# Backward rows out of a Trainium2 kernel: one plain DMA on SyncE's queue in place of an indirect scatter from GpSimd

## The chip, the cores and the metric

The kernel runs on one core of a Trainium2 chip. The metric is device time in microseconds (us); the kernel before was timed three times. The profile is one further look at the same program: one execution recorded by the hardware profiler, with every instruction's start and length, every DMA packet's, and the marks that a DMA's semaphore receives as parts of it land.

## The reference

Two layers in float32. The first is a Fourier mixing of x with 8 batches, 3136 positions and 256 features; the second is a feed-forward layer with a SoLU activation and a layer norm.

```python
X = np.fft.fft(x, axis=1)            # x: (8, 3136, 256)
X = np.fft.fft(X, axis=2).real
h = X.reshape(25088, 256) @ w_in     # w_in: (256, 1024)
e = np.exp(h - h.max(-1, keepdims=True))
solu = h * e / (e.sum(-1, keepdims=True) + 1e-9)
mu, var = solu.mean(-1, keepdims=True), solu.var(-1, keepdims=True)
out = ((solu - mu) / np.sqrt(var + 1e-6) * g_ln) @ w_out   # w_out: (1024, 256)
```

The output is (25088, 256) float32, so a row of it is 1,024 contiguous bytes.

## The kernel before

**Tiling.** 3136 positions are split as 49 x 64: an output position is k1 + 49 * k2, with k1 below 49 and k2 below 64. Since the input is real, k1 and 49 - k1 share their work. A *unit* (p, k1) stands for a pair p of two batches and one k1 from 0 to 24: there are 4 x 25 = 100 units. A unit makes two output tiles of 128 rows (two batches times 64 values of k2): side 0 has the rows of k1, side 1 the rows of 49 - k1. On side 1 the rows of each batch come out with k2 running backwards. Units with k1 = 0 have only side 0, so there are 100 tiles of side 0 and 96 of side 1.

**A unit's way through the engines.** PE makes the second transform (`transform2`), ACT copies it to `q` (`take2`), and a small DMA on SyncE's queue (SP) turns one row of `q` into the column `r` (`spread`, L247). PE multiplies by `Wi` into two PSUM tiles (`up`, L264). DVE combines them to h for both sides (`even`, `join`), ACT takes the exponential and the sum of squares, DVE the product, and DVE transposes u in blocks of 32 x 32 (`turn_both`, L336). For every two units, 16 DMAs on SP move these blocks to their places in the tile `uT` (`move_blocks`, L365; two buffers of `uT`, each for two units). POOL builds four sums of blocks of `uT` (`sums`, L394), and PE makes the second matmul out of seven block products (`Down`, L401): in the order of the code p1, p4, p5, p6, p2, p3, p7.

**The last step of a unit.** The two output tiles are `ot[0]` and `ot[1]`, 128 x 256 each, from a pool with six buffers, which is three units' worth (L417). ACT writes `ot[1]` first (`keep_p`, L435, from the PSUM bank that holds p4 and p5; p3 then adds to that bank), then the two halves of `ot[0]` (L444, L447). DVE finishes both (`finish`, L457 and L459). `store` sends them out: side 0 by a plain DMA on SP (L483), side 1 by an indirect DMA on POOL (L479), which takes the 128 row numbers from the table `idx`.

**The order.** The schedule is written out by hand: every engine's queue runs in the order of the code. One pass i of the main loop (from L828) works on several units at once: unit i enters, unit i - 1 gets its statistics, unit i - 5 goes through `Down` (`lag = 5`), unit i - 6 is stored (`kept`). The pieces of a pass that end up on SP's or POOL's queue are, in this order:

```python
if kept: store(kept, 0)                  # SP
second_transform(i + 2)                  # its spread: SP
other_pairs(i, ahead_pe)                 # in some passes a zd store: SP
other_pairs(i, ahead, "mirror")          # POOL
sums(units[i + 1 - lag], prv)            # POOL
if i % 2 == 0: move_blocks(...)          # 16 DMAs: SP
power(prv)                               # POOL
if kept and 1 in kept.signs: store(kept, 1)   # POOL
other_pairs(i, ahead, "load")            # x of the next pair: SP and POOL
```

So SP takes, over two passes, 16 moves, two stores of side 0, two spreads, and in the first three pairs now and then a `zd` store (L216) and a load of x (L117). The moves of a batch of two units need a free `uT` buffer, which PE gives free after product p2 of an earlier unit. The framework inserts the waits; the eight semaphores of SP's DMAs are used in turn, and each DMA on SP waits for the one eight places ahead of it, whose semaphore it takes over. The framework also orders writes to the same tensor that may touch the same rows; the indirect DMA may touch any row of the output, and the two lines with `declare_no_dep` and `add_to_no_dep_group` tell it that side 0 and side 1 never collide.

Of the kernel before, what the change touches and what calls it, by code (L numbers as in the profile page):

```python
# [20 lines left out]
N1, N2 = 49, 64  # L21
NK = N1 // 2 + 1
# [4 lines left out]
NC = NH // CH  # L27
# [8 lines left out]
def kernel(  # L36
# [19 lines left out]
    nc = tc.nc  # L56
    B, S, D = x.shape
# [3 lines left out]
    NP = B // 2  # L61
# [27 lines left out]
    idx = const.tile([P, NP * (NC + NK - 1)], I32, name="idx")  # L89
# [385 lines left out]
    def store(t, s):  # L475

        if s:
            i = NP * NC + t.p * (NK - 1) + t.k1 - 1
            dma = nc.gpsimd.indirect_dma_start(  # L479
                out=out, out_offset=bass.IndirectOffsetOnAxis(ap=idx[:, i : i + 1], axis=0),  # L480
                in_=t.ot[s], in_offset=None)
        else:
            dma = nc.sync.dma_start(out=out_k[t.p, t.k1], in_=t.ot[s])  # L483

        tc.declare_no_dep(dma.ins, group=f"out{1 - s}", reason="other rows of the output")
        tc.add_to_no_dep_group(f"out{s}", dma.ins)

# [181 lines left out]
    with tc.manual_schedule():  # L671
# [156 lines left out]
        for i in range(whole + 1, len(units) + lag + 1):  # L828
# [6 lines left out]
            if kept:  # L835
                store(kept, 0)
# [44 lines left out]
            if kept and 1 in kept.signs:  # L881
                store(kept, 1)
# [95 lines left out]
```

## Time and profile before

| | us |
|---|---|
| median of three runs | 1170.85 (1168.57 to 1172.88) |
| the profiled execution's own time | 1172.88 |
| its span, first to last instruction | 1171.0 |
| PE busy | 1115.0 (95%) |
| DVE busy | 1022.6 (87%) |
| POOL busy | 868.2 (74%) |
| ACT busy | 757.5 (65%) |
| side 1's stores on POOL, L479 | 115.6 in 96 instructions, 1.204 each |
| side 0's stores on SP, L483 | 100 issues, median 0.570 |
| q1 (DMAs from SP): time of the packets | 60.9% of 16 engines' span |
| q0 (DMAs from POOL): time of the packets | 12.5% of 16 engines' span |

The first row is what a change is compared with; the rows below it belong to one execution, whose own time is 2.0 us above the median. A share of busy time is a mean over the whole span: which engine sets the pace has to be read stage by stage. SP has no busy time of its own in the page, since issuing a DMA doesn't count as work; its rows are found in the timeline as SPq. A DMA's issue and its landing are two events: the rows of SP tell of the issue, the marks on the DMA's semaphore of the landing.

### The profile page before, as it was taken

What the parts mean: (1) busy time and instruction counts of PE and PEld (TensorE: products, weight loads), DVE (VectorE), ACT (ScalarE), POOL (GpSimd) and SP (SyncE); (2) the same over time, 40 slices, a digit from 0 to 9 for tenths busy, and PEclk for the clock granted to TensorE, in tenths of its full rate; (3) what the DMA queues carried; (4) which work ended last, traced back from release to release, by engine and by line L of the source; (5) the groups of instructions that cost most, each with busy time, mean ns of one, the idle gap of its engine ahead of it and who ended that gap; (6) DMA issues with size and microseconds to landing.
All of it is one profiled execution on the core that took longest, in us unless ns stands there. A gap on an engine that the chain in (4) does not pass through costs nothing. (4 is left out here: it accounts for less than half of the span.)

```text
span 1171.0 us, 21594 instructions
## 1 busy us (share of the span) xinstructions
PE 1115.0 (95%) x7002; PEld 891.1 (76%) x7002; DVE 1022.6 (87%) x1428; ACT 757.5 (65%) x1721; POOL 868.2 (74%) x750
## 2 busy tenths in 40 slices
PE   2987999999999999999999999999999999999996
PEld 1555787787787777778878777878878788888886
DVE  7889989888999989999899999888898998998860
ACT  4566666667666666667666766676666666666651
POOL 3035888874998797887688889876598687777675
PEclk9999999999999989999999999999999999999998
DMA  9672798866897969886869797976596675956653
GB/s 240 197 190 45 168 186 186 196 144 145 157 182 155 186 149 174 170 174 143 161 133 202 156 190 164 205 174 144 134 168 154 130 161 113 165 120 134 137 120 93
DMA packets 458479, 185.75 MB, mean 159 GB/s; under 512 B 425750, under 2 KB 440350, under 8 KB 458368
## 3 DMA queue, kind: packets, MB, share of 16 engines
q1 hardware_dynamic: 444608, 146.22, 60.9%
q0 software_dynamic: 13760, 38.16, 12.5%
q8 instruction: 57, 0.93, 0.3%
q14 instruction: 54, 0.44, 0.1%
HBM read 44.78 MB, written 38.80 MB: 71 GB/s over the span
## 5 line engine op out<-in xcount | busy, mean ns | idle before, releaser
L264 PE MATMUL ps_h<-Wi,q 128*128 128x512 f32 x800 | 363.6, 596 | 11.4 <-DVE ev L270 5.9
L394 POOL TENSOR_TENSOR S<-uT 128x512 f32<-128x512 f32 x190 | 258.4, 1360 | 102.1 <-DMA r<-q 39.2
L300 ACT ACTIVATE h<-u,usum 128x1024 f32<-128x1024 f32 x196 | 225.2, 1149 | 155.8 <-DVE u L293 155.8
L401 PE MATMUL ps_m<-Ws,S 128*128 128x128 f32 x2280 | 297.3, 277 | 5.7 <-POOL S L394 3.3
L401 PEld LDWEIGHTS ps_m<-Ws,S 128*128 128x128 f32 x2280 | 280.0, 193 | 10.1 <-POOL S L394 3.7
L264 PEld LDWEIGHTS ps_h<-Wi,q 128*128 128x128 f32 x800 | 144.3, 191 | 160.0 <-issue 141.7
L293 DVE SCALAR_TENSOR_TENSOR u<-h,u 128x1024 f32<-128x1024 f32 x196 | 261.0, 1367 | 0.4 <-ACT u L286 0.3
L286 ACT ACTIVATE u<-h,nmax 128x1024 f32<-128x1024 f32 x196 | 223.7, 1143 | 19.3 <-DVE nmax L278 14.6
L336 DVE STREAM_TRANSPOSE v<-u 128x2048 f32<-128x2048 f32 x93 | 215.4, 2316 | 3.2
L401 PE MATMUL ps_m<-Wo,uT 128*128 128x128 f32 x1520 | 210.9, 282 | 0.0
L401 PEld LDWEIGHTS ps_m<-Wo,uT 128*128 128x128 f32 x1520 | 195.2, 197 | 0.9 <-issue 0.9
L394 POOL TENSOR_TENSOR S<-uT,S 128x512 f32<-128x512 f32 x95 | 134.9, 1420 | 7.4
L278 DVE CUSTOM_DVE_ANT_0 h<-ev,ps_h 128x1024 f32<-128x1024 f32 x100 | 122.1, 1221 | 18.1 <-DVE ev L270 7.4
L479 POOL DMA_INDIRECT out_dram<-ot,idx x96 | 115.6, 1204 | 29.4 <-issue 19.1
L394 POOL TENSOR_TENSOR S<-S,uT 128x512 f32<-128x512 f32 x95 | 129.1, 1359 | 7.5
L278 DVE CUSTOM_DVE_ANT_0 h<-h,ps_h 128x1024 f32<-128x1024 f32 x96 | 117.2, 1221 | 14.2 <-DVE nmax L278 0.5
L270 DVE SCALAR_TENSOR_TENSOR ev<-w_mid,r,ps_h 128x1024 f32<-128x1024 f32 x100 | 124.0, 1240 | 4.1 <-ACT S L530 2.6
L316 POOL TENSOR_TENSOR rs<-v,neg_half 128x2 f32<-128x2 f32 (+1 forms) x100 | 85.8, 858 | 32.3 <-ACT v L309 27.0
L401 PE MATMUL ps_m<-Ws,uT 128*128 128x128 f32 x760 | 105.0, 281 | 0.0
L208 PE MATMUL ps_m<-y,F 98*100 98x258 f32 (+3 forms) x288 | 73.8, 392 | 30.4 <-DVE y L154 23.1
L401 PE MATMUL ps_m<-Wo,S 128*128 128x128 f32 x760 | 100.9, 276 | 0.0
L236 PEld LDWEIGHTS ps_m<-T,g 128*128 128x128 f32 x400 | 60.2, 191 | 48.8 <-issue 46.0
(92 smaller groups left out, 1175.8 us busy)
## 6 DMA issues: line engine op xcount, KB each, us to landing
uT<-v SPq DMA_DIRECT2D x752, 128.0 KB
out_dram<-ot SPq DMA_DIRECT2D x100, 128.0 KB
g<-zd POOLq DMA_DIRECT2D x72, 160.0 KB, 5.2
xa<-in_x_dram SPq DMA_DIRECT2D x28, 392.0 KB
zd<-z SPq DMA_DIRECT2D x24, 400.0 KB
raw_in<-in_moe_w_in_dram SPq DMA_DIRECT2D x4, 512.0 KB
raw_out<-in_moe_w_out_dram SPq DMA_DIRECT2D x2, 1024.0 KB
r<-q SPq DMA_DIRECT2D x100, 0.5 KB
```

The costliest lines, as they stand in the source:

```text
L208: nc.tensor.matmul(o[..., cs], F[:, 2 * t + h, :], i[..., cs], start=first, stop=True, skip_group_check=True)
L264: nc.tensor.matmul(ps[:, fs], t.q[:, c * P : (c + 1) * P], Wi[:, c, fs], start=True, stop=True)
L270: nc.vector.scalar_tensor_tensor(out=t.ev, in0=w_mid, scalar=t.r, in1=ps, op0=ALU.mult, op1=ALU.add)
L278: nc.vector.tensor_tensor_reduce(out=t.h[s], in0=t.h[0] if s else t.ev, in1=t.odd, scale=1.0 if s else -0.5, scalar=3.0e38, op0=ALU.add, o ...
L286: nc.scalar.activation(out=t.u[s], in_=t.h[s], func=ACT.Exp, bias=t.nmax[:, s : s + 1], scale=-1.0, accum_out=t.esum[:, s : s + 1])
L293: t.last = nc.vector.scalar_tensor_tensor(out=t.u[s], in0=t.h[s], scalar=-1.0, in1=t.u[s], op0=ALU.mult, op1=ALU.mult, accum_out=t.usum[:, ...
L300: nc.scalar.activation(out=t.h[s], in_=t.u[s], func=ACT.Square, bias=t.usum[:, s : s + 1], scale=-float(FF), accum_out=t.ssq[:, s : s + 1])
L316: nc.gpsimd.tensor_tensor(out=t.rs[:, n], in0=t.v[:, n], in1=neg_half[:, n], op=ALU.pow)
L336: nc.vector.transpose(out=t.batch.v[:, t.w].rearrange("p f o -> p o f"), in_=t.both)
L394: i = nc.gpsimd.tensor_tensor(out=S[j], in0=a, in1=b, op=op)
L401: nc.tensor.matmul(o, a[:, c], b[:, c], start=start and c == 0, stop=c == n - 1, skip_group_check=True)
L479: dma = nc.gpsimd.indirect_dma_start(out=out, out_offset=bass.IndirectOffsetOnAxis(ap=idx[:, i : i + 1], axis=0), in_=t.ot[s], in_offset=None)
```

## The change

Side 1's tile no longer leaves by an indirect DMA on POOL with a table of rows. It leaves by a plain DMA on SP, whose destination is a view of the output with the dimensions (batch, k2 backwards, feature), that is 2 x 64 x 256 with a negative step in the middle. The two declarations on the order of writes are gone. Nothing else in the program differs; `store(kept, 1)` is called at the same place in the pass.

```diff
     def store(t, s):
 
         if s:
-            i = NP * NC + t.p * (NK - 1) + t.k1 - 1
-            dma = nc.gpsimd.indirect_dma_start(
-                out=out, out_offset=bass.IndirectOffsetOnAxis(ap=idx[:, i : i + 1], axis=0),
-                in_=t.ot[s], in_offset=None)
+            o = out.rearrange("(b k2 k1) d -> k1 b k2 d", b=B, k1=N1)[N1 - t.k1, 2 * t.p : 2 * t.p + 2, ::-1, :]
+            dma = nc.sync.dma_start(out=o, in_=t.ot[s])
         else:
             dma = nc.sync.dma_start(out=out_k[t.p, t.k1], in_=t.ot[s])
 
-        tc.declare_no_dep(dma.ins, group=f"out{1 - s}", reason="other rows of the output")
-        tc.add_to_no_dep_group(f"out{s}", dma.ins)
```

## The prediction, made before the changed kernel was run

> **What bounds the kernel now.** I read the table by stage first, because the shares of the page are means over the whole span.
>
> ```profile
> 0.00:100.00 100.00, 69.87 (x256) 42.10 (x257) 81.93 (x147) 58.41 (x106) 23.91 (x29) 1.00 0.69 184
> ...
> 300.00:400.00 100.00, 98.75 (x634) 79.47 (x633) 94.73 (x119) 67.22 (x155) 87.30 (x73) 1.00 0.90 172
> 400.00:500.00 100.00, 93.90 (x586) 76.09 (x585) 91.06 (x121) 61.76 (x146) 84.40 (x68) 0.97 0.79 165
> ...
> 1000.00:1100.00 100.00, 100.00 (x658) 80.87 (x657) 89.48 (x119) 68.88 (x154) 72.07 (x59) 1.00 0.65 133
> ```
>
> The columns are PE, PEld, DVE, ACT, POOL, the clock and the DMA share. PE is busy 93.9 to 100 us of every 100 between 100 and 1100 us; its idle time there adds up to 15.4 us over all ten rows. So nothing that frees POOL can be worth more than 15 us, while whatever delays PE counts in full. The rows on POOL and the waits say how much of the 15 us is POOL's:
>
> ```profile
> L479 POOL DMA_INDIRECT out_dram<-ot,idx x96 | 115.6, 1204 | 29.4 <-issue 19.1 <-DMA out_dram<-ot,idx 6.9 <-DVE nmax L278 2.4
> PE ps_m L401 <- POOL S L394: 3.3, 2, 2.7
> SPq L365 <- PE ps_m L401: 91.7, 43, 3.5
> ```
>
> PE waited for POOL's sums 3.3 us in the whole run (PEld 3.7 us), in two waits, the longer (2.7 us) at 1149 us. The third row says that in 43 of the 48 sets the moves begin when PE gives `uT` free: SP is ready before. Then I read one cycle of two units in the timelines of SP, POOL, ACT and PE:
>
> ```profile
> 971.10 13.93 SPq L365 DMA_DIRECT2D uT<-v  x16
> 985.14 0.58 SPq L483 DMA_DIRECT2D out_dram<-ot  x1
> 985.82 0.53 SPq L247 DMA_DIRECT2D r<-q  x1
> 986.45 0.54 SPq L483 DMA_DIRECT2D out_dram<-ot  x1
> 987.46 0.53 SPq L247 DMA_DIRECT2D r<-q  x1
> 991.66 2.06 SPq L365 DMA_DIRECT2D uT<-v  x2
> ...
> 987.68 1.51 POOL L394 TENSOR_TENSOR S<-uT 128x512 f32<-128x512 f32 x1 [4.75 <-DMA out_dram<-ot]
> ...
> 989.84 0.47 ACT L435 ACTIVATE ot<-ps_m,rs 128x256 f32<-128x256 f32 x1 [0.91 <-POOL S L394]
> ...
> 991.42 1.06 PE L401 MATMUL ps_m<-Wo,S 128*128 128x128 f32 x8
> ```
>
> Of the 20.6 us from one set of moves to the next, SP issues for 16.1 us and has 3.7 us to spare ahead of the next set. POOL stood idle 4.75 us until the last move had landed (its mark is at 987.5; the wait is put down to another DMA of the queue). PE uses these sums about 9 us later, so this wait costs nothing.
>
> **POOL's part.** 96 instructions of 1.204 us leave POOL: 115.6 us off a queue that bounds no stage. Worth on the path: 0 at least; at most the 3.3 + 3.7 us of waits for sums, and less where those sums waited for a landing. I take 3 us, with 10 us as the outer end. At the tail, the last scatter starts 1.8 us after its tile is ready (ACT ends at 1165.35, L479 starts at 1167.12), since it waits for the one before. A plain DMA needs no such wait, but lands later (below): 0 to 2 us, I take 1.
>
> **SP's part.** Two issues more per cycle at 0.57 us, the median of L483: 1.1 us, beside 3.7 us to spare. In the first three pairs a cycle is 22.3 us, with room for it too. Behind them in the queue are `r` (read two passes later) and the stores of side 0. So the issues cost nothing; if SP had no room, it would be 48 x 1.1 = 53 us.
>
> **How the transfer itself runs** is what decides, and the trace of before has no such DMA. Each DMA's semaphore shows how many engines it uses: 16 separate marks for 128 rows (L483) and for the 32 rows of a move; for the 100 rows of a `zd` store one early mark and then ten; for the 98 rows of an x load one and then fourteen. [...] The new destination has 2 outermost, for it can't be merged with a backward step; the source has 128 partitions. If the 2 decides, two engines carry 64 rows each; if the source decides, 16 carry 8 each. I take two. [...]
>
> In the trace's packet records 1,024-byte packets on q1 take 46 ns at the median, 75 ns at the 90th percentile. 64 of them one after another are 2.94 us on each of two engines (4.8 us at 75 ns; 1.5 us if two are always in flight, as the count of up to 30 packets on 16 engines allows). From the last packet's end to the last mark it is 0.43 us (the store at 1157.6). They queue behind the last move on these engines.
>
> **Where that lands on the path.** In an even pass `store(kept, 1)` stands behind the 16 moves. Today POOL issues it during them (973.5 in the cycle shown). It reads `ot[1]` of unit u, and with six buffers the tile of unit u + 3 is the same memory: `keep_p` (L435) has to wait for the landing, and PE's p3 (the row at 991.42) for `keep_p`. In the cycle shown: the last move lands at 987.5, so its packets end about 987.1; plus 2.94 plus 0.43 is 990.5. `keep_p` slips from 989.84 to 990.5 and ends at 991.0, before p3 at 991.42: nothing lost, by 0.4 us. In the set that begins at 566.16, issue ends at 582.28 and the last move lands at 588.4, because POOL's loads of g (L224, at 568.9 and 578.6) run beside it: 588.0 + 2.94 + 0.43 + 0.47 + 0.1 = 591.9 against p3 at 586.48, so PE loses 5.4 us. I worked this out for the 44 sets that have such a pair: 27 lose nothing, three up to 0.5, fourteen 1.5 to 5.4 us, together 37 us. With 1.5 us for the transfer it is 16 us, with 4.8 us 87 us. In an odd pass the store leaves early in the pass, one unit ahead of its reuse: nothing.
>
> Both stores of a cycle lie ahead of the next moves: 5.9 us of packets from about 987.1, against the first packets of the next set about 992.7: hidden here. Where sets follow within 5 us (582.3 to 586.7, 624.7 to 629.0, and others in the last third of each pair), the first moves land up to 3 us later, and with eight semaphores in turn SP slows once landings take more than about 7 us. If that ends every set 1 us later, the sum over the sets is 60 instead of 37 us; I take 6 us of these 23.
>
> **Sum.** +37 + 6 - 3 - 1 = +39 us: 1172.9 becomes 1212 in the profiled execution, and since that stands 2.0 us above the median, 1170.85 becomes **1210 us** (+3.3%). With the ends: 16 - 10 - 2 = +4 to 87 + 23 = +110, so 1175 to 1281.
>
> **Rivals.**
> - *Sixteen engines, so not slower.* If the source's 128 partitions set the spread, the store lands 2.4 to 3.8 us after its issue (the quiet stores of L483, and their median): 985.14 + 3.8 = 988.9, ahead of `keep_p` at 989.84. Then only the gains are left, -3 and -2 at the tail: 1166 us, with 1159 as the end. It decides if the landing stays under about 4.7 us behind the last move. For it: a scatter with 4.1 us to landing stands there today and hurts nobody. Against it: the pattern of the marks.
> - *Two engines as the bound.* The page has 60.9 + 12.5 = 73.4% of all engines' time in packets. Less the scatter's 4.1 (a third of q0's bytes), plus 96 x 64 x 46 ns = 283 us on two engines (24.1% of the span), these two stand at 93% in the mean and 111% in the stage from 300 to 400 us. Moves, which use all 16, would run at their pace: 10 us more in that stage at 46 ns; at 75 ns about 95 us over the stages above 0.75. With the main sum: 1220 to 1305, I say 1260. For it: in the set from 566.16, with the share at 1.13 between 576 and 590 us, a move took 7 us to land instead of 3.3. Against it: a share above 1 is possible at all, since packets overlap in an engine.
> - *Stores that wait for each other.* Without the declarations each store might wait for the one before it, if the framework can't see that backward rows and forward rows never meet. Behind the moves stand side 1, side 0, side 1, side 0: 5.4 + 3.8 + 4.4 us of landings, so the next moves begin about 14 us after the set instead of 6.6 (last pair) or 9: 12 x 7.4 + 35 x 5 = 264 us, 1435 us. Against it: today's stores of side 0 go to interleaved rows, and the one at 709.7 us is issued before that of 706.4 has landed (4.1 us).
>
> **Chances.** Main case 0.55, sixteen engines 0.20, two engines as the bound 0.15, waiting stores 0.10. A run tells about 0.5% (6 us) from no change. The 0.20 splits into 0.09 faster and 0.11 same; the low end of the main case adds 0.01 same, the rest of it and the others are slower: 0.09, 0.12, 0.79. The range leaves out the waiting stores (0.10), the end of the bound case (0.05) and the better part of the first rival (0.05): 1163 to 1275. The main case alone has 1175 to 1281.
>
> **What would show it.** Right: the new DMA has one early mark and two late ones; 1,024-byte packets on q1 double in number; q0 loses its scatter; ACT L435 waits for a DMA of `ot`, and PE's L401 for ACT L435, mostly where loads of g or x run beside the moves; POOL falls by some 115 us. Wrong: sixteen marks per new DMA (first rival); moves whose landings grow through the whole set (second); SP rows of L483 waiting 4 to 5 us for a DMA (third); or PE idle elsewhere.

## The result, and the profile after

The changed kernel takes 1211.78 us (median of four runs, 1206.87 to 1216.63) against 1170.45 us: a ratio of 1.0352 with a 95% interval of 1.0305 to 1.0399. The prediction had 1210 us and slower at 0.79. The number came out; the two terms that carried it were both off, as the experiments show.

The page after, busy times and the two queues:

```profile
PE 1122.1 (93%) x7002; PEld 895.1 (74%) x7002; DVE 1010.7 (83%) x1428; ACT 755.0 (62%) x1721; POOL 742.3 (61%) x654
...
q1 hardware_dynamic: 457088, 158.80, 62.9%
q0 software_dynamic: 9152, 25.57, 9.3%
```

POOL lost 125.9 us, 115.6 of them the scatters', and q0 lost its scatters. The span grew by 40.0 us: PE's busy time by 7.1, its idle time by 32.9. The table by stage (columns as before) shows where:

```profile
200.00:300.00 100.00, 99.75 (x651) 81.11 (x650) 86.99 (x130) 67.87 (x160) 57.24 (x48) 1.00 0.67 151
300.00:400.00 100.00, 88.52 (x529) 70.30 (x529) 73.50 (x100) 55.76 (x127) 62.38 (x58) 0.93 0.74 148
...
800.00:900.00 100.00, 91.95 (x595) 75.26 (x595) 78.73 (x116) 61.33 (x145) 60.22 (x55) 0.97 0.74 154
900.00:1000.00 100.00, 99.05 (x631) 79.12 (x631) 88.11 (x111) 66.32 (x151) 57.92 (x52) 1.00 0.69 139
1000.00:1100.00 100.00, 100.00 (x658) 80.87 (x657) 90.09 (x120) 69.60 (x158) 62.67 (x54) 1.00 0.69 134
```

The stages that lose most are 300 to 400 us (88.5 us busy where it was 98.8) and 800 to 900, whose row before was this:

```profile
800.00:900.00 100.00, 99.85 (x665) 81.92 (x665) 89.61 (x117) 66.02 (x156) 77.20 (x66) 1.00 0.72 145
```

From 1000 to 1100 us, in the last pair, PE is as busy as it was. The waits after the change, PE's and those of ACT and SP beside it, say what the time is lost for:

```profile
ACT ot L444 <- DMA out_dram<-ot: 43.9, 19, 5.1
PE ps_m L401 <- ACT ot L444: 16.5, 11, 3.5
PE ps_m L236 <- DMA g<-zd: 14.2, 2, 7.1
PE ps_m L208 <- ACT q L242: 11.3, 7, 2.1
...
SPq L365 <- PE ps_m L401: 43.8, 24, 3.4
```

The columns are total us, times, longest. The first two rows are one chain: ACT waits with `keep_x` (L444) for a store to land, and PE's p7 waits for ACT. The third was not in the profile of before at all: twice PE stands 7.1 us for g, the input of the second transform. The fourth was 6.7 us. The last row is slack: only 24 of the 48 sets of moves still find SP waiting for PE; it was 43.

The first chain at one place, in the timelines of ACT and PE:

```profile
187.38 0.37 ACT L444 ACTIVATE ot<-ps_m,rs 128x128 f32<-128x128 f32 x1 [4.30 <-DMA out_dram<-ot]
...
187.89 1.41 PE L401 MATMUL ps_m<-Ws,S 128*128 128x128 f32 x8 [2.70 <-ACT ot L444]
```

The side 1 store issued at 177.98 has its last mark at 187.29, 0.09 us before ACT goes on. In all 20 places where ACT waits over 1 us at L444, a side 1 store's last mark stands 0.08 to 0.09 us ahead of ACT's start; it is the store of the unit three before. Each of these stores has one early mark and two late ones (this one at 179.34, 187.18 and 187.29): two engines.

### The profile page after: what moved, and what is told of

Its sections match the earlier page's. It is cut to its first block, busy times and chain, and to the rows that moved or that the text cites. A ratio compares the mean times of both kernels' runs of the same rounds, so it can differ in the third digit from the quotient of the medians.

```text
span 1211.0 us, 21609 instructions
## 1 busy us (share of the span) xinstructions
PE 1122.1 (93%) x7002; PEld 895.1 (74%) x7002; DVE 1010.7 (83%) x1428; ACT 755.0 (62%) x1721; POOL 742.3 (61%) x654
## 4 chain that ended last, share of the span: by engine, by line
PE 52%; DMA 17%; SPq 16%; DVE 7%; issue 4%; POOL 2%; ACT 2%; DVEq 0%; POOLq 0%; ACTq 0%
PE ps_m L401 29%; PE ps_h L264 16%; SPq L365 15%; DMA out_dram<-ot 8%; PE ps_m L208 3%; DVE u L293 2%; POOL S L394 2%; PE ps_m L236 2%; DMA xa<-in_x_dram 2%; DMA room<-in_x_dram 2%; DMA uT<-v 2%; DMA g<-zd 1%; DMA r<-q 1%; DVE h L278 1%; PE ps_m L468 1%
## 5 line engine op out<-in xcount | busy, mean ns | idle before, releaser
L394 POOL TENSOR_TENSOR S<-uT 128x512 f32<-128x512 f32 x190 | 254.0, 1337 | 210.3 <-DVE u L293 51.4
L264 PE MATMUL ps_h<-Wi,q 128*128 128x512 f32 x800 | 367.8, 602 | 8.8 <-DVE ev L270 4.5
L401 PE MATMUL ps_m<-Ws,S 128*128 128x128 f32 x2280 | 296.7, 276 | 18.2 <-ACT ot L444 16.5
L401 PEld LDWEIGHTS ps_m<-Ws,S 128*128 128x128 f32 x2280 | 278.7, 193 | 23.8 <-POOL S L394 12.9
L264 PEld LDWEIGHTS ps_h<-Wi,q 128*128 128x128 f32 x800 | 146.8, 194 | 159.1 <-issue 144.9
L293 DVE SCALAR_TENSOR_TENSOR u<-h,u 128x1024 f32<-128x1024 f32 x196 | 245.7, 1288 | 0.5 <-ACT u L286 0.3
L401 PE MATMUL ps_m<-Wo,uT 128*128 128x128 f32 x1520 | 211.8, 283 | 0.6 <-DMA uT<-v 0.6
L401 PEld LDWEIGHTS ps_m<-Wo,uT 128*128 128x128 f32 x1520 | 196.0, 198 | 1.7 <-issue 1.7
L394 POOL TENSOR_TENSOR S<-uT,S 128x512 f32<-128x512 f32 x95 | 126.3, 1329 | 7.4
L278 DVE CUSTOM_DVE_ANT_0 h<-h,ps_h 128x1024 f32<-128x1024 f32 x96 | 117.2, 1221 | 14.2 <-ACT y L167 0.5
L394 POOL TENSOR_TENSOR S<-S,uT 128x512 f32<-128x512 f32 x95 | 124.1, 1306 | 7.5
L134 POOL TENSOR_TENSOR xa<-xa,xb 98x510 f32<-98x510 f32 (+1 forms) x48 | 59.7, 1246 | 98.5 <-DMA xa<-in_x_dram 52.9
L457 DVE SCALAR_TENSOR_TENSOR ot<-ps_m,rs,ot 128x128 f32<-128x128 f32 x95 | 33.2, 350 | 93.2 <-PE ps_m L401 52.9
L316 POOL TENSOR_TENSOR rs<-v,neg_half 128x2 f32<-128x2 f32 (+1 forms) x100 | 89.4, 894 | 34.8 <-ACT v L309 29.6
L401 PE MATMUL ps_m<-Ws,uT 128*128 128x128 f32 x760 | 106.2, 283 | 0.0
```

The lines of the kernel that those rows point to most:

```text
L264: nc.tensor.matmul(ps[:, fs], t.q[:, c * P : (c + 1) * P], Wi[:, c, fs], start=True, stop=True)
L278: nc.vector.tensor_tensor_reduce(out=t.h[s], in0=t.h[0] if s else t.ev, in1=t.odd, scale=1.0 if s else -0.5, scalar=3.0e38, op0=ALU.add, o ...
L293: t.last = nc.vector.scalar_tensor_tensor(out=t.u[s], in0=t.h[s], scalar=-1.0, in1=t.u[s], op0=ALU.mult, op1=ALU.mult, accum_out=t.usum[:, ...
L316: nc.gpsimd.tensor_tensor(out=t.rs[:, n], in0=t.v[:, n], in1=neg_half[:, n], op=ALU.pow)
L394: i = nc.gpsimd.tensor_tensor(out=S[j], in0=a, in1=b, op=op)
L401: nc.tensor.matmul(o, a[:, c], b[:, c], start=start and c == 0, stop=c == n - 1, skip_group_check=True)
```

## Experiments

Every ratio is to the kernel before on the same chip. Landings are medians from issue to last mark.

**e1: forwards, sixteen engines.** Same queue, same place; only the destination changes.

```diff
-            o = out.rearrange("(b k2 k1) d -> k1 b k2 d", b=B, k1=N1)[N1 - t.k1, 2 * t.p : 2 * t.p + 2, ::-1, :]
+            o = out_k[t.p, N1 - t.k1]
```

> The changed kernel with side 1's rows leaving forwards: same queue, same place in it, same bytes, but a destination of 128 rows in one dimension. The rows of side 1 end up in the mirrored places within their batch, so that part of the output is changed. Theory N (two engines carry the whole transfer): sixteen landing marks per store, no wait of L444 for a store over 1 us, no wait of PE for g, time 1164 to 1175 us. Rival Q (the place behind the moves on SP's queue is what costs, not the number of engines): the store is issued as late as in the changed kernel, so L444 waits and time stays at 1195 to 1212 us.

Measured: 1162.99 us, ratio 0.9933 [0.9907, 0.996]. So neither SP's two issues nor the place behind the moves costs anything worth the name, and the same store on sixteen engines is a small gain. ACT's waits at L444 for a store fall from 43.9 to 2.6 us (the longest is 1.2, a little over the 1 us expected), and PE's waits for g are gone. What the narrow form costs is 1211.78 - 1162.99 = 49 us. The stores in both profiles (shortest, median and longest issue in ns), e1 first, then the changed kernel:

```profile
L481 SPq DMA_DIRECT2D out_dram<-ot x100: 332/449/3232, 111.0 to 1156.8; - x100
L479 SPq DMA_DIRECT2D out_dram<-ot x96: 333/589/2817, 135.4 to 1160.2; - x96
```

```profile
L481 SPq DMA_DIRECT2D out_dram<-ot x100: 338/816/3034, 109.6 to 1200.7; - x100
L479 SPq DMA_DIRECT2D out_dram<-ot x96: 511/583/1212, 133.1 to 1204.1; - x96
```

Read the row that was not changed. Side 0's store (L481) has sixteen engines in both kernels, yet its issue takes 816 ns at the median instead of 449, and it lands after 6.4 us instead of 3.2. It stands behind the narrow store. Its 16 marks tell where the time goes. In the changed kernel the fourteenth mark comes 4.0 us after the issue and the fifteenth 6.1 us after it (medians); in e1 it is 2.8 and 2.9. In 85 of the 100 stores of side 0 the last two marks come over 1 us behind the fourteenth, in e1 in none. The same holds for 62 of the 100 transfers of `r` (L247), in e1 again for none. So two engines of the sixteen hold up transfers that the change does not touch.

**e2: the same transfer from POOL's queue.**

```diff
-            dma = nc.sync.dma_start(out=o, in_=t.ot[s])
+            dma = nc.gpsimd.dma_start(out=o, in_=t.ot[s])
```

> The changed kernel with the same backward plain DMA issued by POOL instead of SP, at the place where the scatter stood. Issue leaves the queue behind the moves, the narrow transfer stays. Theory N: about 64 rows per engine still run for 3 us on two engines each time, so the waits for g and for late moves stay and the time is 1185 to 1205 us. Rival Q: the store is early again, 1160 to 1173 us. POOL should lose some 0.6 us per store against the scatter (1.204 to about 0.6 us).

Measured: 1246.86 us, ratio 1.0648 [1.0617, 1.0678]. Worse than both expectations. SP's order is not the cause, but the transfer is not the same one either: each store now has 16 marks and 224 packets of 16 bytes besides its data, and a set of moves takes 21.4 us from its first issue to its last landing (17.7 before, 18.4 after). As a test of the two engines it says little.

**e3: the narrow store at the head of the pass**, behind side 0's and ahead of the moves.

```diff
             if kept:
                 store(kept, 0)
+                if 1 in kept.signs:
+                    store(kept, 1)
```

> The changed kernel with side 1's store issued right behind side 0's at the head of the pass, so ahead of the moves; still narrow, still on SP. L444's wait for the buffer should be gone under both theories. Theory N: two engines carry 64 rows ahead of zd, moves and r, so the waits for g stay; 1185 to 1203 us. Rival Q: 1165 to 1175 us.

Measured: 1218.32 us, ratio 1.0404 [1.0374, 1.0433]: both expectations missed, and nothing gained over the changed kernel. ACT's waits at L444 for a store are gone (0.8 us), but PE now waits 26.3 us for `q` and 17.5 us for g.

**e4: eight `ot` buffers instead of six**, which takes away what the prediction's main term rests on. Room comes from the part of `idx` that the plain store does not need.

```diff
-    idx = const.tile([P, NP * (NC + NK - 1)], I32, name="idx")
+    idx = const.tile([P, NP * NC], I32, name="idx")
...
-            t.ot = [fpool.tile([P, D], FP32, tag="ot", name="ot", bufs=6) for _ in range(2)]
+            t.ot = [fpool.tile([P, D], FP32, tag="ot", name="ot", bufs=8) for _ in range(2)]
...
```

> The changed kernel with eight output buffers instead of six (and a table idx cut to the columns still in use, to make room), so a store has one unit more to land. Only the buffer wait goes: the 16.5 us that PE waited for L444 and what follows from it. If the buffer wait and the wait for g are separate, 1188 to 1198 us with the two 7 us waits for g still there; if the buffer wait is the root of all, 1166 to 1178 us; if it costs nothing by itself, 1207 to 1214 us.

Measured: 1217.87 us, ratio 1.0389 [1.0353, 1.0426], above the highest of the three expectations. Its waits:

```profile
PE ps_m L208 <- ACT q L242: 21.6, 14, 3.1
PE ps_m L236 <- DMA g<-zd: 16.9, 2, 9.1
...
ACT ot L444 <- PE ps_m L401: 33.1, 92, 1.1
```

No row of L444 waiting for a store is left, so the edit did what it should, and the time did not fall. PE loses the same in other places: its waits over 0.15 us add up to 80.4 us here, to 81.2 in the changed kernel. The buffer wait is where the delay showed, not where it came from.

**e5, e6, e7: direction against number of engines.** Three destinations for side 1, all else as after.

```diff
 e5  forwards, 2 x 63 rows
+            o = out.rearrange("(b k2 k1) d -> k1 b k2 d", b=B, k1=N1)[N1 - t.k1, 2 * t.p : 2 * t.p + 2, 0 : N2 - 1, :]
+            dma = nc.sync.dma_start(out=o, in_=t.ot[s][0 : P - 2])
 e6  backwards, 16 x 8 rows
+            o = out.rearrange("(g c k1) d -> k1 g c d", c=8, k1=N1)[N1 - t.k1, 16 * t.p : 16 * t.p + 16, ::-1, :]
 e7  backwards, 4 x 32 rows
+            o = out.rearrange("(g c k1) d -> k1 g c d", c=32, k1=N1)[N1 - t.k1, 4 * t.p : 4 * t.p + 4, ::-1, :]
```

> Side 1's rows go forwards, but as 2 batches x 63 rows (the last row of each batch is left out and the rows that are written stand in the wrong order), so that the two counts can't be merged. N, the theory that the outermost count of 2 puts the store on two engines and that this crowding is what costs: three marks per store and nearly the whole loss of the change, 1205 to 1220 us. B, the rival that the descending addresses cost, whatever the engines: 1159 to 1167 us, like the forward store on sixteen engines (1163).

> Side 1's rows go backwards within 16 groups of 8 rows (the order of the rows is not the reference's), so that the outermost count is 16. N: sixteen marks per store, and the time of the forward store on sixteen engines, 1159 to 1168 us. B: all or most of the loss stays, 1195 to 1220 us.

> Side 1's rows go backwards within 4 groups of 32 rows (order not the reference's): outermost count 4, so by N four engines with 32 packets each. N: a late store and a move held back by half as much, so that a third to a half of the loss of 49 us against the sixteen-engine store stays: 1172 to 1188 us; if slack swallows so short a delay altogether, 1163 to 1170. B: 1195 to 1220 us.

| store of side 1 | us | ratio | marks | side 1 lands | side 0 lands | SP waits for PE |
|---|---|---|---|---|---|---|
| e6, backwards, 16 | 1164.08 | 0.9932 [0.9906, 0.9959] | 16 | 3.7 | 3.3 | 82.2 |
| e7, backwards, 4 | 1192.81 | 1.0159 [1.0111, 1.0206] | 1 + 4 | 5.4 | 4.7 | 56.7 |
| e5, forwards, 2 | 1212.66 | 1.0347 [1.0317, 1.0377] | 1 + 2 | 6.7 | 6.2 | 42.5 |
| after, backwards, 2 | 1211.78 | 1.0352 [1.0305, 1.0399] | 1 + 2 | 6.9 | 6.4 | 43.8 |

(The last column is the row SPq L365 <- PE ps_m L401 of each kernel, in us.) The direction costs nothing, the number of engines all of it. Four engines keep (1.0159 - 0.9932) / (1.0347 - 0.9932) = 55% of the loss (43 to 66% by e7's own interval), where a third to a half was expected. Side 0's marks agree (medians from the issue): with two engines the step stands behind the fourteenth mark, 3.9 and then 6.0 us in e5; with four it stands behind the twelfth, 3.2 and then 3.9 us in e7. e6 writes backwards without the declarations and loses nothing, which does away with the rival of stores that wait for each other. The marks of these runs go with the destination's outermost count, 2 for 2, 4 for 4 and 16 for 16, though the source has 126 or 128 rows. That narrow stores meet on the same two engines is seen at the end of the changed kernel, where SP issues nothing but stores. From 1203.5 us on at most three 1,024-byte packets of 46 ns are under way at once, and two begin every 42 ns. The last marks come in the order of the queue: at 1206.65 for the narrow store issued at 1197.48, at 1206.99 for side 0's of 1200.68, at 1209.69 for the narrow one of 1204.09, and the last 128 packets take 2.9 us. Which two of the sixteen these are, no run shows. The loads at L117, which run on fourteen engines (one early mark and fourteen), end with two marks over 1 us late in 20 of 32 in the changed kernel and in none in e1, so the crowded two are among those fourteen.

**e8: side 1 not stored at all.**

```diff
         if s:
+            return
```

> Side 1's rows are computed but not stored at all (half of the output is not written). N: the issue and the bytes of a well spread store cost next to nothing, so 1153 to 1163 us, at most 10 us below the forward store on sixteen engines. The rival that SP's two more issues and the 12.6 MB more on its queue are a good part of the loss: below 1150 us.

Measured: 1160.36 us, ratio 0.9889 [0.9852, 0.9926]. The whole price of a well spread store (e6 or e1 against e8) is about 0.4%, and the intervals overlap.

**e9: more issues on SP, none of them narrow.** Side 1 forwards, in two DMAs of 64 rows.

```diff
+            o = out_k[t.p, N1 - t.k1]
+            for h in (slice(0, P // 2), slice(P // 2, P)):
+                nc.sync.dma_start(out=o[h], in_=t.ot[s][h])
```

> The forward store on sixteen engines (rows in the wrong order within side 1), cut into two DMAs of 64 rows, so that SP issues four more DMAs per cycle than before instead of two, and no engine is crowded. N (the crowded engines hold up what is queued behind them, and SP's own issues are covered by its slack): 1160 to 1169 us, like the single forward store (1163). S (SP's issue time is the cost: the forward store's 842 us of issues after 100 us become some 895, what the store on four engines had at 1191 us): 1180 to 1192 us.

Measured: 1167.41 us, ratio 0.9981 [0.9962, 1.0]. From 100 us on SP issues for 918 us here, against 843 in e1 and 938 after. So nearly the changed kernel's issue time costs some 5 us over e1, not 49. SP's slack is as small here as there, too: it waits 37.3 us for PE ahead of the moves, against 43.8 after. Neither SP's issue time nor its lost slack costs much by itself.

**e10: the narrow store from ACT's queue.**

```diff
-            dma = nc.sync.dma_start(out=o, in_=t.ot[s])
+            dma = nc.scalar.dma_start(out=o, in_=t.ot[s])
```

> The changed kernel, with side 1's store issued by ScalarE instead of SP; the transfer itself is the same. N: two engines are crowded as before, so SP's moves and zd stores still land late and SP's issues are still stretched: 1195 to 1225 us. S (the order and the room in SP's queue are the cost): 1163 to 1180 us.

Measured: 1577.65 us, ratio 1.3477 [1.3436, 1.3517], far outside both. SP's timeline, and ACT's store:

```profile
484.14 28.38 SPq L365 DMA_DIRECT2D uT<-v  x16
...
504.98 0.52 ACTq L479 DMA_DIRECT2D out_dram<-ot  x1
```

The sixteen moves spread over 28.4 us, of which SP issues for 13.4. The fourteenth starts at 510.58, 0.02 us after ACT's store has landed (510.56), and it uses that store's semaphore. The eight DMA semaphores go round over both queues in the order of the code, so SP waited for a store that ACT reached only at 504.98. The edit brought in a new wait and tells nothing about the two engines.

**e11: forward stores only ahead of the two waits for g.**

```diff
+            if t.p in (0, 2) and 11 <= t.k1 <= 15:
+                o = out_k[t.p, N1 - t.k1]
```

> The changed kernel, with forward stores on sixteen engines for 10 of the 96 units only: k1 = 11 to 15 in pairs 0 and 2, the stores that leave in the 50 us before the last zd store of those pairs (their rows are in the wrong order). If the two 7 us waits of PE for g are a loss with a place of its own: both fall below 1.5 us, and the time to 1194 to 1201 us. If the loss is spread evenly over the 72 stores that cost anything (none is lost in the last pair): 10/72 of 49 us, so 1203 to 1208 us.

Measured: 1195.74 us, ratio 1.0226 [1.0204, 1.0248]: 16 us back for 10 of 96 stores, as a loss with a place of its own predicts. The changed kernel first: SP with the last `zd` store of the pair (L216), POOL with the loads of g that wait for it, PE with the second transform.

```profile
275.72 2.57 SPq L481 DMA_DIRECT2D out_dram<-ot  x1
278.38 0.55 SPq L247 DMA_DIRECT2D r<-q  x1
279.10 15.53 SPq L365 DMA_DIRECT2D uT<-v  x16
294.68 0.58 SPq L479 DMA_DIRECT2D out_dram<-ot  x1
295.39 0.47 SPq L481 DMA_DIRECT2D out_dram<-ot  x1
295.96 0.56 SPq L247 DMA_DIRECT2D r<-q  x1
296.98 0.31 SPq L216 DMA_DIRECT2D zd<-z  x1
297.39 0.59 SPq L479 DMA_DIRECT2D out_dram<-ot  x1
...
302.84 2.44 POOL L224 DMA_DIRECT2D g<-zd  x4 [13.30 <-DMA zd<-z]
...
312.78 1.20 PE L236 MATMUL ps_m<-T,g 128*128 128x128 f32 x4 [7.11 <-DMA g<-zd]
```

Then the same rows of e11, where the stores ahead of and behind this `zd` store are wide:

```profile
281.40 13.34 SPq L365 DMA_DIRECT2D uT<-v  x16
...
297.99 0.30 SPq L216 DMA_DIRECT2D zd<-z  x1
...
302.18 2.44 POOL L224 DMA_DIRECT2D g<-zd  x4 [10.19 <-DMA zd<-z]
...
308.26 0.66 PE L236 MATMUL ps_m<-T,g 128*128 128x128 f32 x4
```

From the `zd` store's issue to POOL's next instruction it is 5.9 us in the changed kernel (296.98 to 302.84) and 4.2 in e11; PE then starts 9.9 us after POOL in the one and 6.1 in the other, without a wait. A `zd` store and the g loads are transfers that the change does not touch. But both seem to have a share on the crowded engines. The `zd` store runs on ten engines (one early mark and ten), and its last mark comes 1.0 us behind the eighth (0.3 in e11); in 9 of 32 `zd` stores of the changed kernel, and in none of e1, the last two marks are over 1 us late. The fourth g load's last mark comes 1.6 us behind its fourteenth (0.1 in e11). The delay is handed on three times: zd, g, PE. That is not all of it: the eighth mark of `zd` comes 1.0 us later after the issue than in e11, and the fourteenth of that load 2.4 us, and why is not shown. The set of moves in between takes 15.5 us instead of 13.3. Note also PE's 1.20 us for four matmuls that take 0.61 to 0.66 elsewhere: the granted clock is low after the stall (0.50 from 308 to 318 us, 0.93 in the stage from 300 us), which is part of the 7.1 us by which PE's busy time grew.

**e12: narrow stores only in the last pair**, scatters elsewhere and for the last unit.

```diff
-        if s:
+        if s and t.p == NP - 1 and t.k1 < NK - 1:
+            o = out.rearrange("(b k2 k1) d -> k1 b k2 d", b=B, k1=N1)[N1 - t.k1, 2 * t.p : 2 * t.p + 2, ::-1, :]
+            dma = nc.sync.dma_start(out=o, in_=t.ot[s])
+            s = 0
+        elif s:
```

> The kernel before, with the backward store on SP's queue only in the last pair (k1 = 1 to 23; the last unit keeps its scatter); the output is the reference's. N (where no x, zd or g moves, there is slack for the crowded engines): nothing lost there, PE's wait of 2.7 us for sums at 1149 us gone and the last scatter free to start when its tile is ready: 1165 to 1171 us. A fixed price per store, 23/96 of the change's 41 us: 1178 to 1183 us.

Measured: 1172.68 us, ratio 1.0026 [1.001, 1.0043]: between the two expectations, 1.7 us above the first and 5.3 below the second. A fixed price per store is out: 23 narrow stores in a stage without `zd`, g and x transfers cost PE nothing. The gain at the end did come, and was given back. PE and POOL at the end of e12:

```profile
1152.91 7.15 PE L468 MATMUL ps_m<-Wo,uT 128*128 128x256 f32 x32 [0.66 <-DVE ot L459]
...
1160.87 1.07 POOL L483 DMA_INDIRECT out_dram<-ot,idx  x1 [10.18 <-ACT ot L473]
```

PE is done at 1160.06, where before it was done at 1164.80, and the scatter's last mark is at 1163.81 (1169.53 before). But the span ends at 1169.99 (1171.02): POOL's closing drain runs from 1160.62 to 1169.21 here and from 1166.90 to 1170.24 before. Why it outlasts the landing by 5.4 us is open. No kernel that gives the reference's rows beat the one before; a last pair without any scatter was not tried.

## Why the prediction was right, and where it was not

**Two engines: right.** The marks are 1 + 2, and the choice between destination and source, on which the sign hung, was the right one. The profile of before had no such DMA to tell which of the two decides; e5, e7 and e6 tell it, with 2, 4 and 16 engines. The transfer was costed at 2.94 us on two engines; a narrow store lands 6.9 - 3.5 = 3.4 us later than a wide one in e1.

**POOL's part and the tail (-4 us): right in sign, small in size.** e1 and e6, with everything but the narrowness, are 0.7% below before, some 8 us; their intervals hold 5 to 11. The first rival's 1166 us was that case. In the changed kernel itself the tail grew instead: from PE's last instruction to the end it takes 7.4 us, against 6.2 before, because the last narrow store lands 5.6 us after its issue (1.7 us in e1, where the tail is 3.5 us).

**SP's issues (0): right.** e1 shows it for two issues a cycle; the two further ones of e9 cost about 5 us.

**The buffer wait (+37 us): the step that failed.** The store lands late and an `ot` buffer comes free late, as worked out. But the wait fell on `keep_x` (L444), which writes `ot[0]`, and on p7 instead of `keep_p` (L435) and p3, and PE lost 16.5 us by it, not 37. And it is no term of a sum: without it (e4) the time is the same or worse. The step treated one late transfer and asked who waits for it. What the marks show is that a DMA on all engines has its share on the two crowded ones and lands with the slowest (side 0's stores in the changed kernel: fourteenth mark after 4.0 us, last after 6.4).

**Moves held back (+6 of 23 us): the right mechanism, undersized and seen in one place only.** Two engines that hold up what runs beside them are the second rival's mechanism, in mild form. A set of moves takes 18.44 us from first issue to last landing, against 17.20 in e1, so 1.24 us more, close to the 1 us that the prediction priced at 23 us and then took a quarter of. What this delay of the moves costs by itself no run separates; PE waits 0.6 us for a move in the whole run. And the step left out the handoff from `zd` to g, where a delay counts in full because PE has nothing else: 16 us by e11. PE's additional idle time of 32.9 us is 16.5 (p7) + 14.2 (g) + 4.6 (more for `q`) + 1.2 (the tail), less the 3.3 us for sums that went away: 33.2. That the total came to 1210 is one term too large and one too small, and so in part luck. Of the 49 us between e1 and the changed kernel e11 places 16 at g. The rest comes from the two engines as well (e5 against e6), but at which wait it arises is open, since p7's 16.5 us only moved when e4 took that wait away.

**Stores that wait for each other: wrong.** In the changed kernel SP never waits over 0.15 us for a DMA ahead of a store; the waits for one that are put down to a store stand ahead of eight moves (4.6 us in all), one `zd` store (0.3 us) and the end of the program. e6 drops the declarations too and is no slower than before.

**The eight semaphores as the reason for slow issues: not so.** For the 138 issues of SP that took over 1.2 us in the changed kernel (after its first 100 us), the DMA that had the semaphore before had always landed when the issue began, by 2.5 us at the median. What such an issue waits for is not shown. The landing time of about 7 us from which the prediction had SP slow down was an estimate (eight issues of 13.93 / 16 = 0.87 us, as in the cycle shown there, take 7.0 us); the changed kernel does not show it as a limit. Where the semaphore does bind, in e10, the wait stands between issues and not in one.

## What to carry to other kernels

Before a scatter is replaced by a plain DMA, count the outermost steps of the destination that can't be merged. Here 2, 4 and 16 of them gave as many engines, and the transfer on two of sixteen delayed not only itself (6.9 us to land instead of e1's 3.5) but the wide transfers queued behind it (6.4 instead of 3.2). Price it at the handoffs where the next engine has no other work (here `zd` to g to PE, 16 us by e11), not at the buffer it releases. If adding buffers takes a wait away and the time stays (1217.87 us in e4 against 1211.78), the wait was where a delay surfaced; look for transfers that the change does not touch and that have become slower.

## What the hardware did that was not expected

- A DMA on sixteen engines that is queued behind a narrow one lands after 6.4 us instead of 3.2, because the last two of its marks come some 2 us behind the other fourteen, and its issue takes 816 ns instead of 449 (medians, after and e1).
- The same plain DMA issued from POOL had 16 marks and 224 extra packets of 16 bytes per store, and cost 1.0648 instead of 1.0352.
- POOL's closing drain lasted 8.6 us with the scatter issued during it (e12), ending 5.4 us after that scatter's last mark; before, with several scatters ahead of it, 3.3 us and 0.7 us.
- With 340 us of PE idle time the mean granted clock fell to 0.889 (e10), against 0.984 after and 0.993 before.
